# The order of side work in a long-convolution and cosine-gated kernel: table Sin in one row, group matrices by turns, and a tile's sums copied ahead of the preceding Sin

## The chip, the cores and the metric

The kernel runs on one core of a Trainium2 chip. The metric is the device time of one execution in microseconds (us), as the median of several runs. A profile of one execution shows each engine's instructions: TensorE (PE for matmuls, PEld for weight loads), VectorE (DVE), ScalarE (ACT), GpSimd (POOL) and the queue that issues all DMAs (SP).

## What is computed

```python
u = x * v                                    # x, v: 4 x 12480 x 128
h = (np.maximum(pos_emb @ w1, 0) @ w2) * np.exp(-0.01 * pos)[:, None]
y = np.fft.irfft(np.fft.rfft(u, n=2*S, axis=1) * np.fft.rfft(h, n=2*S, axis=0)[None], axis=1)[:, :S]
z = (x * y).reshape(49920, 128)
g = z @ w_in;  g = g * np.cos(g)             # w_in: 128 x 2048
out = g @ w_out                              # w_out: 2048 x 128
```

All is computed in float32. The two gate weights come as float64 and are turned into float32 on the chip.

## The kernel before

**The convolution** is a transform of length 2 x 96 x 120 in two factors, written as matmuls with tables of sines. Its stages are named f1 and f2 (forward), i1 and i2 (inverse). A stage is a Python generator (`units`, L527): for each unit it issues the matmuls, then piece by piece the work that takes the unit before out of PSUM, and the preparation (`before`) of a coming unit. The order in which the instructions are issued is thus written out by hand: the program advances generators in turn (`next`), and every engine carries out its own instructions in exactly that order. A wait at the head of an engine's order holds up all that stands behind it.

**The first 345 us**, up to the first tile of the second part, run in this order:

- the filter h, and its f1 (64 units, matmuls L407, taken out of PSUM by ACT and DVE by turns);
- `first_f1`, the f1 of batch 0: 64 units, evicted by ACT (L415, L423, L425) or DVE;
- `f2_both_units` (L607), the f2 of filter and batch 0 at once: 48 units. Each makes a matrix pair w (`make_w`: ACT L294 scales one term, DVE L296 adds the other), stores it in DRAM (wd) for the later batches, does the matmuls L448 to L454, copies the filter's half out (ACT L633, h), stores that as well (hd), multiplies (DVE L467) and adds (L474, on POOL, but on DVE for the last pair);
- the i1 of batch 0: 64 units, matmuls L479, ACT copies one half (L487, `other`), DVE adds and subtracts it (L489).

Beside them stands work that has to be done some time: the tables of the inverse (`inverse_tables`, L253; POOL computes an argument `turned`, L218, ACT takes its Sin, L227, and the tables are stored as csd, rowsd and twd), the conversion of w_in and w_out to float32 (`convert_units`, L168), and six of the thirty groups of inverse matrices (`some_groups`, L667). PSUM has eight banks in these stages, which units take in turn.

The `Tables` helper lets Sin lag behind their arguments: with a lag of 11 it holds 12 buffers `turned`, and only when 11 arguments wait is the first Sin issued. What is left at the end is issued one Sin at each further step. The steps are driven by f1 and then first_f1, one table step for every fourth of their steps (L873 to L878), so that the last Sin stand between evictions of first_f1.

`beside` (L884) runs the units of a stage, with a convert step at every tenth step (w_in, during first_f1) or every twelfth (w_out, during i1), and a step of `some_groups` where the number of the step modulo 9 is 1 or 5. In front of first_f1 the program advances `f2` once: w of unit 0 is made and stored there, in a pool of its own on the right side.

**The inverse's matrices.** A group is four matrices (`make_group`, L656). A matrix is the sum of two terms: ACT makes the first term (L294); then either DVE multiplies and adds the second (L296), or ACT makes the second into a buffer `spare` (L299) and POOL adds (L300). For the i2 of batch 0, 24 groups are made in the flow, one group ahead, one matrix in each of a unit's four parts: the first two by DVE, the other two by POOL, with one buffer `spare`. The first half of a unit's matmuls (L504) uses the first two matrices. The groups are stored (td) and loaded again by the later batches (`tm<-td`).

**The second part** starts when the first rows of z are there. 98 tiles of up to 512 tokens go through 16 chunks of 128 hidden columns each. For a chunk, `moe_up` (L749) does one matmul into a bank `ph` (L752), ACT makes `a` (L755), DVE rounds it to `k` (L758), POOL subtracts (`f`, L761); `moe_act` (L764) takes the Sin (`cs`, ACT L766) and multiplies by ph (`gt`, DVE L768); `moe_down` (L771) multiplies gt with w_out into the tile's sums `acc` (L777). After a tile's last chunk `moe_evict` copies the sums to `ot` (ACT L783), which is transposed (L127), copied to `ob` (L792) and stored. There are four ph banks and one acc bank; when the convolution is done, odd tiles use another bank (`cv`). The loop (L939 to L961) issues at step i: moe_up of chunk i, moe_act of chunk i - 1, moe_down of chunk i - 4 and, at a tile's end, moe_evict. The rest of the convolution, i2 of batch 0 and then f1, f2, i1, i2 of batches 1 to 3, is fed into the same loop by a budget (`owed`): one step of cost 1 per chunk.

Of the kernel before, what the change touches and what calls it, by code (L numbers as in the profile page):

```python
# [3 lines left out]

# [6 lines left out]
F32 = mybir.dt.float32  # L11
U32 = mybir.dt.uint32
AF = mybir.ActivationFunctionType
# [18 lines left out]
def kernel(  # L32
# [46 lines left out]
    nc = tc.nc  # L79
# [4 lines left out]
    N1, N2 = 96, 120  # L84
    R = S // N2
# [166 lines left out]

    def inverse_tables(pool):  # L253

        t = Tables(pool, nc.gpsimd, 11)
        part = t.whole([P, 1], [[1, 1]], channel_multiplier=1, name="part")
        part4 = t.whole([P, 1], [[1, 1]], base=1, channel_multiplier=4, name="part4")
        step = t.whole([P, P], [[1, P]], name="step")
        mid = t.whole([P, P], [[1, P]], base=-MID, name="mid")
        cs, (rows, tw_t) = third_table(pool), last_tables(pool)  # L260
        yield from t.sines(step, part, N2, [(cs[:, 0, 0:H + 1], 1), (cs[:, 1, 0:H + 1], 0)],
                           eighths=slice(0, H + 1, H))
        yield from t.sines(step[:, 1:H], part, N2,
                           [(cs[:, 0, H + 1:], 0), (cs[:, 1, H + 1:], 1)])
        yield from t.sines(step, part4, 4 * N1,
                           [(rows[:, i, :], q) for i, q in enumerate((0, 1, 2, 3))])
        yield from t.sines(mid, part4, TURN, [(tw_t[:, 0, :], 1), (tw_t[:, 1, :], 0)],
                           eighths=slice(H - 1, N2, H))
        while t.waiting:
            t.finish(1)  # L270
            yield
        for kept, made in ((csd, cs), (rowsd, rows), (twd, tw_t)):
            nc.sync.dma_start(kept[:, :, :], made[:, :, :])

# [27 lines left out]
    def make_w(w, k1, **how):  # L302


        turn(w, even[:, 0, :], even[:, 1, :], tw_w[:, 0, k1:k1 + 1], tw_w[:, 1, k1:k1 + 1],
             **how)
# [149 lines left out]
    def f2_product(pool, ps, h, k1, whole, sums=nc.gpsimd):  # L456
# [12 lines left out]
        for r, op in ((0, ALU.subtract), (1, ALU.add)):  # L469
            if not whole:  # L470
                nc.vector.tensor_tensor(y[:, r], uu[:, 0], h[:, r], op=ALU.mult)
                yield
                nc.vector.tensor_tensor(t[:, r], uu[:, 1], h[:, 1 - r], op=ALU.mult)
            sums.tensor_tensor(y[:, r], y[:, r], t[:, r], op=op)  # L474
            yield

    def i1_mm(ps, b, i):
# [126 lines left out]
            yield from units(N1 // 2, F2_STEPS, before, mm,  # L604
                             lambda j, ps: f2_product(pool, ps, hs.pop(j), 2 * j, False), 4)

    def f2_both_units(bank, w_pool):  # L607

        ws, unkept = {}, []

        def before(j):
            ws[j] = w_pool.tile([KE, 2, N2], F32, name="w")
            for i in range(2):
                make_w(ws[j][:, i, :], 2 * j + i, half=bank)
            unkept.append(j)
            if j < 2:
                keep_w()

        def keep_w():
            while unkept:  # L620
                k = unkept.pop(0)
                nc.sync.dma_start(wd[k, :, :, :], ws[k][:, :, :])

        def mm(j, ps, i):
            if i == 0:
                ps = bank(), bank()
            for filt in range(2):
                f2_mm(ps[filt], ws[j], 2 * j, i, filt=filt == 1)
            return ps

        def after(j, ps):
            h = pool.tile([N2, 2, CB, 4], F32, name="h", bufs=3)
            nc.scalar.activation(h[:, :, :, :].rearrange("p r b j -> p (r b j)"),  # L633
                                 ps[1][0:N2, :], AF.Copy, scale=1.0 / M)
            nc.sync.dma_start(hd[j, :, :, :, :], h[:, :, :, :])
            keep_w()
            yield from f2_product(pool, ps[0], h, 2 * j, True,
                                  nc.vector if 2 * j + 2 == N1 else nc.gpsimd)

        steps = units(N1 // 2, F2_STEPS, before, mm, after, 4, ahead=1)  # L640
        yield next(steps)
        with tc.tile_pool(name="both", bufs=2) as pool:
            yield from steps

    def i1_units(bank):
        with tc.tile_pool(name="mid", bufs=2) as pool:
# [9 lines left out]
    def make_group(pool, g, t, summed, bufs=1):  # L656

        for i, n2 in enumerate(n2s(g)):
            if i < G - summed:
                make_t(t[:, i, :, :], n2)  # L660
            else:
                spare = pool.tile([N1, 2, R], F32, name="spare", bufs=bufs)
                make_t(t[:, i, :, :], n2, spare=spare[:, :, :])
            yield
        nc.sync.dma_start(td[g, :, :, :, :], t[:, :, :, :])

    def some_groups(pool):  # L667
        for g in SOME:
            t = pool.tile([N1, G, 2, R], F32, name="some", bufs=2)
            yield from make_group(pool, g, t, G, bufs=2)  # L670
            if g == SOME[-2]:
                next(backs[0])

    def i2_units(bank, b, bufs):

# [133 lines left out]
    with tc.manual_schedule():  # L809
        with tc.tile_pool(name="psum", bufs=8, space=PSUM) as psum, \  # L810
                ExitStack() as first:
            def bank():
                return psum.tile([P, BANK], F32, name="ps")
# [58 lines left out]
            keep.__exit__(None, None, None)  # L872
            with tc.tile_pool(name="tables", bufs=1) as pool:  # L873
                sines = inverse_tables(pool)
                first_f1 = f1_units(bank, slots[0:R, :, :, :], 0.55)
                for i, _ in enumerate(chain(f1, first_f1)):
                    if i % 4 == 0 and next(sines, "made") == "made":
                        break  # L878

            backs = [inverse_units(lambda: bank(), b) for b in range(B)]

            def beside(units, pieces, every, more=lambda pool: iter(())):  # L884
                with tc.tile_pool(name="convert", bufs=1) as pool:
                    convert, other = convert_units(pool, pieces), more(pool)
                    for i, _ in enumerate(units):
                        if i % every == 0:
                            next(convert, None)
                        elif i % 9 in (1, 5):  # L890
                            next(other, None)
                    for _ in [*convert, *other]:
                        pass

            w_pool = first.enter_context(tc.tile_pool(name="w", bufs=2, side="right"))
# [6 lines left out]
            for _ in f2:  # L902
                pass
            first.close()

# [11 lines left out]
            beside(i1_units(bank), [(w_out_sb[:, c, :], w) for c, w in out_pieces], 12, some_groups)  # L917
# [29 lines left out]
        for i in range(len(steps) + LAG):  # L947
            if i < len(steps):
                n, c = steps[i]
                if n == 0 and c == NFC // 2:  # L950
                    load(1)
                if c == NFC - 4 and n + 2 < NALL:
                    load(n + 2)
                hidden[i] = moe_up(mpool, n, c)
            if 0 <= i - 1 < len(steps):
                gates[i - 1] = moe_act(mpool, *hidden.pop(i - 1))
            if i >= LAG:
                pn, pc = steps[i - LAG]
# [12 lines left out]
            while owed > 0.0:  # L971
                owed -= next(conv, owed)
# [30 lines left out]
```

## Time and profile before

| | |
|---|---|
| median of three runs | 3789.84 us (3787.87 to 3790.01) |
| profiled execution | 3789.84 us, of which the span from the first to the last instruction is 3788.0 us |
| busy: PE, PEld | 3701.4 us (98%), 2105.1 us |
| busy: DVE, ACT, POOL | 2768.3, 2520.8, 2594.0 us |
| mean granted TensorE clock | 0.996 |
| chain that ended last, by engine | PE 81%, POOL 6%, DVE 3%, ACT 2%, DMA 2% |
| DMA | 276.14 MB, mean 73 GB/s |

In the profile, L752 is line 752 of the kernel before. An arrow `cs<-f` names the tile written and the tiles read. Idle time of an engine is put down to what ended it: `PE acc L777 <- ACT ot L783: 9.6, 15, 1.5` means that in 15 places, 9.6 us together and 1.5 us at most, TensorE stood still before an instruction of L777 until ACT had finished an instruction of L783. In the timeline a line gives the start, the time taken, engine, line, operation, tiles and shapes, and in brackets the idle time before. The granted clock is the share of full speed that TensorE got.

### The profile page before, as it was taken

Reading aid. Unit: us, or ns where it says so; the run is one execution under the profiler, and the core shown is the slowest. Engines: PE = TensorE matmul, PEld = TensorE weight load, DVE = VectorE, ACT = ScalarE, POOL = GpSimd, SP = SyncE. Lnnn points to the kernel's source line nnn. Section 1 sums busy time; section 2 is a strip of 40 time slices with the busy share of each in tenths; the row PEclk is TensorE's granted clock in tenths of the full one; section 3 lists DMA queues with packets and bytes.
Section 4 is the critical chain, followed back from the end, with each engine's and each line's share of the span. In section 5 each row is a group of like instructions: output and inputs, shape, how many; then the busy total and the mean of one; then the engine's idle time right before and its main releaser. Section 6 shows DMA issues by size and latency. Waiting matters only on the chain.

```text
span 3788.0 us, 47204 instructions
## 1 busy us (share of the span) xinstructions
PE 3701.4 (98%) x13546; PEld 2105.1 (56%) x13546; DVE 2768.3 (73%) x5564; ACT 2520.8 (67%) x4683; POOL 2594.0 (68%) x2340
## 2 busy tenths in 40 slices
PE   7898999999999999999999999999999999999999
PEld 6776555655466555555565556555566544444444
DVE  7887887688766777778767786788765566666666
ACT  5756776766665557766655567666664677777777
POOL 7666886588854665688745664788644577777776
PEclk9999999999999999999999999999999999999999
DMA  6253452022202651122203540122105300000000
GB/s 166 67 180 100 147 151 60 16 73 76 77 18 66 178 161 27 32 77 77 60 18 109 173 127 18 51 78 76 41 12 164 90 18 22 17 19 21 17 21 14
DMA packets 209498, 276.14 MB, mean 73 GB/s; under 512 B 17111, under 2 KB 146535, under 8 KB 209111
## 3 DMA queue, kind: packets, MB, share of 16 engines
q1 hardware_dynamic: 209239, 273.12, 24.7%
q8 instruction: 109, 1.79, 0.2%
q14 instruction: 150, 1.23, 0.1%
HBM read 193.64 MB, written 79.42 MB: 72 GB/s over the span
## 4 chain that ended last, share of the span: by engine, by line
PE 81%; POOL 6%; DVE 3%; ACT 2%; DMA 2%; issue 2%; SPq 0%; POOLq 0%; DVEq 0%; ACTq 0%
PE ph L752 31%; PE acc L777 26%; PE cv L777 5%; PE cv L504 4%; PE cv L479 4%; POOL f L761 4%; PE cv L407 3%; PE cv L448 3%; PE ph L127 2%; PE ps L448 1%; DMA tm<-td 1%; ACT cs L766 1%; POOL tm L300 1%; DVE k L758 1%; DVE slots L489 1%
## 5 line engine op out<-in xcount | busy, mean ns | idle before, releaser
L761 POOL TENSOR_TENSOR f<-a,k 128x512 f32<-128x512 f32 (+1 forms) x1568 | 1989.0, 1269 | 1055.0 <-DVE k L758 1054.0
L752 PE MATMUL ph<-at,w_in_sb 128*128 128x512 f32 (+1 forms) x3136 | 1598.5, 591 | 5.9 <-DVE gt L768 5.2
L755 ACT ACTIVATE a<-ph,quarter 128x512 f32<-128x512 f32 (+1 forms) x1568 | 1073.3, 685 | 751.7 <-PE ph L752 742.3
L777 PE MATMUL acc<-gt,w_out_sb 128*128 128x512 f32 (+1 forms) x2688 | 1374.1, 593 | 10.0 <-ACT ot L783 9.6
L768 DVE TENSOR_TENSOR gt<-ph,cs 128x512 f32<-128x512 f32 (+1 forms) x1568 | 1077.8, 687 | 319.2 <-ACT cs L766 291.7
L758 DVE TENSOR_SCALAR k<-a 128x512 f32<-128x512 f32 (+1 forms) x1568 | 770.3, 491 | 618.0 <-ACT a L755 598.4
L766 ACT ACTIVATE cs<-f 128x512 f32<-128x512 f32 (+1 forms) x1568 | 980.4, 625 | 338.7 <-POOL f L761 336.3
L777 PEld LDWEIGHTS acc<-gt,w_out_sb 128*128 128x128 f32 x2688 | 505.2, 189 | 663.0 <-issue 619.0
L752 PEld LDWEIGHTS ph<-at,w_in_sb 128*128 128x128 f32 x3136 | 553.5, 190 | 338.2 <-issue 267.0
L474 POOL TENSOR_TENSOR slots<-slots,t 120x256 f32<-120x256 f32 x382 | 309.9, 817 | 63.0 <-DVE t L467 30.8
L504 PEld LDWEIGHTS cv<-slots,tm 96*104 96x104 f32 x1920 | 239.5, 170 | 109.4 <-issue 83.8
L504 PE MATMUL cv<-slots,tm 96*104 96x128 f32 x1920 | 253.7, 274 | 9.7 <-DMA tm<-td 4.9
L777 PE MATMUL cv<-gt,w_out_sb 128*128 128x512 f32 (+1 forms) x448 | 224.5, 583 | 0.7 <-DVE gt L768 0.7
L479 PEld LDWEIGHTS cv<-cs,slots 120*96 120x96 f32 x1536 | 177.5, 168 | 68.0 <-issue 66.1
L479 PE MATMUL cv<-cs,slots 120*96 120x120 f32 x1536 | 183.9, 266 | 0.0
L448 PE MATMUL cv<-slots,w 124*120 124x256 f32 x576 | 173.0, 380 | 0.0
L448 PEld LDWEIGHTS cv<-slots,w 124*120 124x120 f32 x576 | 103.6, 184 | 123.8 <-issue 110.9
L407 PEld LDWEIGHTS cv<-c,slots 104*124 104x124 f32 x768 | 132.5, 192 | 71.2 <-issue 58.3
L407 PE MATMUL cv<-c,slots 104*124 104x192 f32 x768 | 151.2, 326 | 4.8 <-DVE gt L768 3.5
L777 PEld LDWEIGHTS cv<-gt,w_out_sb 128*128 128x128 f32 x448 | 84.9, 190 | 104.5 <-issue 99.5
L395 DVE TENSOR_TENSOR xt<-xt,vt 104x256 f32<-104x256 f32 x177 | 139.1, 793 | 0.8 <-DMA vt<-in_v_dram 0.8
L489 DVE TENSOR_TENSOR slots<-cv,other 96x240 f32<-96x240 f32 x384 | 133.7, 394 | 4.2 <-ACT other L487 4.2
(130 smaller groups left out, 2569.5 us busy)
## 6 DMA issues: line engine op xcount, KB each, us to landing
h<-hd SPq DMA_DIRECT2D x144, 240.0 KB
tm<-td SPq DMA_DIRECT2D x96, 312.0 KB
xt<-in_x_dram SPq DMA_DIRECT2D x120, 208.0 KB
vt<-in_v_dram SPq DMA_DIRECT2D x120, 208.0 KB
xs<-in_x_dram SPq DMA_DIRECT2D x120, 208.0 KB
zd<-zs SPq DMA_DIRECT2D x119, 208.0 KB
zb<-zd SPq DMA_DIRECT2D x96, 256.0 KB
w<-wd SPq DMA_DIRECT2D x144, 116.2 KB
```

The costliest lines, as they stand in the source:

```text
L407: nc.tensor.matmul(ps[0:KE, i * 2 * N1:(i + 1) * 2 * N1], u[:, b, 0:KE, i], c1[0:u.shape[0], :, :].rearrange("p r k -> p (r k)"), start=Tr ...
L448: nc.tensor.matmul(pi, w[:, i, :], parts[0:KE, :, k], start=True, stop=True)
L474: sums.tensor_tensor(y[:, r], y[:, r], t[:, r], op=op)
L479: nc.tensor.matmul(ps[0:N1, (i * 2 + r) * N2:(i * 2 + r + 1) * N2], parts[0:N2, r, :, b, i], cs[:, r, :], start=True, stop=True)
L504: nc.tensor.matmul(ps[0:R, i * D:(i + 1) * D], t[:, i, r, :], slots[0:N1, :, place, :], start=(r == 0), stop=(r == 1))
L752: nc.tensor.matmul(ph[:, 0:m], w_in_sb[:, c * P:(c + 1) * P], ats[n][:, 0:m], start=True, stop=True)
L755: nc.scalar.activation(a[:, 0:m], ph[:, 0:m], AF.Identity, bias=quarter[:, 0:1], scale=INV_TWO_PI)
L758: nc.vector.tensor_scalar(out=k[:, 0:m], in0=a[:, 0:m], scalar1=ROUND, scalar2=ROUND, op0=ALU.add, op1=ALU.subtract)
L761: nc.gpsimd.tensor_tensor(f[:, 0:m], a[:, 0:m], k[:, 0:m], op=ALU.subtract)
L766: nc.scalar.activation(cs[:, 0:m], f[:, 0:m], AF.Sin, scale=TWO_PI)
L768: nc.vector.tensor_tensor(gt[:, 0:m], ph[:, 0:m], cs[:, 0:m], op=ALU.mult)
L777: nc.tensor.matmul(accs[n][:, 0:m], w_out_sb[:, c, :], gt[:, 0:m], start=(c == 0), stop=(c == NFC - 1))
```

## The change

TensorE's instructions keep their order throughout the kernel. What moves is work of the other engines:

1. The inverse tables' lag is 4 instead of 11, with 5 buffers `turned`. The last four Sin are issued in one row. Only f1 drives the steps, every fifth of its steps; the steps left over are all issued behind the last step that f1 yields, and its last two units are evicted behind those; first_f1 follows.
2. w of f2's unit 0 is made at the start of f2, behind first_f1, in the pool of f2's other tiles, again with two buffers. Each w is stored as soon as it is made, ahead of the store of h of the unit before; before, from the third w on, behind it.
3. POOL does the sums L474 of f2's last pair as well.
4. In `beside` a convert step comes at every fourteenth step, and a step of `some_groups` at every fifth. Group 0 of batch 0's i2 is made behind the last of `some_groups`; before, it was made ahead of the last of them.
5. The matrices of a group alternate: DVE, POOL, DVE, POOL. There are two buffers `spare`.
6. In the second part's loop moe_down of chunk i - 4 and the copy of a tile's sums stand ahead of moe_act of chunk i - 1.

```diff
     def inverse_tables(pool):
-        t = Tables(pool, nc.gpsimd, 11)
+        t = Tables(pool, nc.gpsimd, 4)
...
-        while t.waiting:
-            t.finish(1)
-            yield
+        t.finish(len(t.waiting))
...
-            sums.tensor_tensor(y[:, r], y[:, r], t[:, r], op=op)
+            nc.gpsimd.tensor_tensor(y[:, r], y[:, r], t[:, r], op=op)
...
-    def f2_both_units(bank, w_pool):
-        ws, unkept = {}, []
-        def before(j):
-            ws[j] = w_pool.tile([KE, 2, N2], F32, name="w")
-            for i in range(2):
-                make_w(ws[j][:, i, :], 2 * j + i, half=bank)
-            unkept.append(j)
-            if j < 2:
-                keep_w()
+    def f2_both_units(bank):
+        with tc.tile_pool(name="both", bufs=2) as pool:
+            ws = {}
+            def before(j):
+                ws[j] = pool.tile([KE, 2, N2], F32, name="w")
+                for i in range(2):
+                    make_w(ws[j][:, i, :], 2 * j + i, half=bank)
+                nc.sync.dma_start(wd[j, :, :, :], ws[j][:, :, :])
...
-            if i < G - summed:
+            if summed < G and i % 2 == 0:
                 make_t(t[:, i, :, :], n2)
             else:
-                spare = pool.tile([N1, 2, R], F32, name="spare", bufs=bufs)
+                spare = pool.tile([N1, 2, R], F32, name="spare", bufs=2)
                 make_t(t[:, i, :, :], n2, spare=spare[:, :, :])
...
-            yield from make_group(pool, g, t, G, bufs=2)
-            if g == SOME[-2]:
-                next(backs[0])
+            yield from make_group(pool, g, t, G)
+        next(backs[0])
...
-                first_f1 = f1_units(bank, slots[0:R, :, :, :], 0.55)
-                for i, _ in enumerate(chain(f1, first_f1)):
-                    if i % 4 == 0 and next(sines, "made") == "made":
-                        break
+                for i, _ in enumerate(f1):
+                    if i % 5 == 0:
+                        next(sines, None)
+                for _ in sines:
+                    pass
...
-                        if i % every == 0:
+                        if i % 14 == 0:
                             next(convert, None)
-                        elif i % 9 in (1, 5):
+                        elif i % 5 == 0:
                             next(other, None)
...
-            f2 = f2_both_units(bank, w_pool)
-            next(f2)
-            beside(first_f1, [(wind[:, c], w) for c, w in in_pieces], 10)
+            beside(f1_units(bank, slots[0:R, :, :, :], 0.55),
+                   [(wind[:, c], w) for c, w in in_pieces])
...
                 hidden[i] = moe_up(mpool, n, c)
-            if 0 <= i - 1 < len(steps):
-                gates[i - 1] = moe_act(mpool, *hidden.pop(i - 1))
             if i >= LAG:
                 pn, pc = steps[i - LAG]
                 moe_down(pn, pc, gates.pop(i - LAG))
                 if pc == NFC - 1:
                     ots[pn] = moe_evict(mpool, pn)
+            if 0 <= i - 1 < len(steps):
+                gates[i - 1] = moe_act(mpool, *hidden.pop(i - 1))
```

More of the change, by code (lines that the diff above doesn't have):

```diff
@@ L2 @@
 from contextlib import ExitStack
-from itertools import chain
 import concourse.bass as bass
@@ L454, in f2_mm, with f2_product @@
                 nc.tensor.matmul(pi[:, r], w[:, i, :], src, start=True, stop=True)
-    def f2_product(pool, ps, h, k1, whole, sums=nc.gpsimd):
+    def f2_product(pool, ps, h, k1, whole):
         y = parts[0:N2, :, k1:k1 + 2, :, :].rearrange("p r k b i -> p r b (k i)")
@@ L605, in f2_units @@
                              lambda j, ps: f2_product(pool, ps, hs.pop(j), 2 * j, False), 4)
-    def f2_both_units(bank, w_pool):
-        ws, unkept = {}, []
-        def before(j):
-            ws[j] = w_pool.tile([KE, 2, N2], F32, name="w")
-            for i in range(2):
-                make_w(ws[j][:, i, :], 2 * j + i, half=bank)
-            unkept.append(j)
-            if j < 2:
-                keep_w()
[L619 to L641, printed above, removed]
-        with tc.tile_pool(name="both", bufs=2) as pool:
-            yield from steps
@@ new lines, in f2_both_units, with mm, after @@
+    def f2_both_units(bank):
+        with tc.tile_pool(name="both", bufs=2) as pool:
+            ws = {}
[4 more added lines that the diff above has]
+                nc.sync.dma_start(wd[j, :, :, :], ws[j][:, :, :])
+            def mm(j, ps, i):
+                if i == 0:
+                    ps = bank(), bank()
+                for filt in range(2):
+                    f2_mm(ps[filt], ws[j], 2 * j, i, filt=filt == 1)
+                return ps
+            def after(j, ps):
+                h = pool.tile([N2, 2, CB, 4], F32, name="h", bufs=3)
+                nc.scalar.activation(h[:, :, :, :].rearrange("p r b j -> p (r b j)"),
+                                     ps[1][0:N2, :], AF.Copy, scale=1.0 / M)
+                nc.sync.dma_start(hd[j, :, :, :, :], h[:, :, :, :])
+                yield from f2_product(pool, ps[0], h, 2 * j, True)
+            yield from units(N1 // 2, F2_STEPS, before, mm, after, 4, ahead=1)
@@ L654, in i1_units, with make_group @@
                              lambda j, ps: i1_evict(pool, ps, j), 2)
-    def make_group(pool, g, t, summed, bufs=1):
+    def make_group(pool, g, t, summed):
         for i, n2 in enumerate(n2s(g)):
-            if i < G - summed:
+            if summed < G and i % 2 == 0:
                 make_t(t[:, i, :, :], n2)
             else:
-                spare = pool.tile([N1, 2, R], F32, name="spare", bufs=bufs)
+                spare = pool.tile([N1, 2, R], F32, name="spare", bufs=2)
                 make_t(t[:, i, :, :], n2, spare=spare[:, :, :])
@@ L874, with beside @@
                 sines = inverse_tables(pool)
-                first_f1 = f1_units(bank, slots[0:R, :, :, :], 0.55)
-                for i, _ in enumerate(chain(f1, first_f1)):
-                    if i % 4 == 0 and next(sines, "made") == "made":
-                        break
+                for i, _ in enumerate(f1):
[3 more added lines that the diff above has]
+                    pass
             backs = [inverse_units(lambda: bank(), b) for b in range(B)]
-            def beside(units, pieces, every, more=lambda pool: iter(())):
+            def beside(units, pieces, more=lambda pool: iter(())):
                 with tc.tile_pool(name="convert", bufs=1) as pool:
@@ L893, in beside @@
                         pass
-            w_pool = first.enter_context(tc.tile_pool(name="w", bufs=2, side="right"))
-            f2 = f2_both_units(bank, w_pool)
-            next(f2)
-            beside(first_f1, [(wind[:, c], w) for c, w in in_pieces], 10)
+            beside(f1_units(bank, slots[0:R, :, :, :], 0.55),
+                   [(wind[:, c], w) for c, w in in_pieces])
             lpool = ctx.enter_context(tc.tile_pool(name="late", bufs=1))
@@ L901 @@
             nc.sync.dma_start(cs[:, :, :], csd[:, :, :])
-            for _ in f2:
+            for _ in f2_both_units(bank):
                 pass
@@ L916 @@
             nc.sync.dma_start(w_in_sb[:, :], wind[:, :])
-            beside(i1_units(bank), [(w_out_sb[:, c, :], w) for c, w in out_pieces], 12, some_groups)
+            beside(i1_units(bank), [(w_out_sb[:, c, :], w) for c, w in out_pieces], some_groups)
         ps_acc = ctx.enter_context(tc.tile_pool(name="ps_acc", bufs=1, space=PSUM))
```

## The prediction, made before the changed kernel had run

> **What bounds the kernel now.** I read the page first (busy shares, then the chain of work that ended last), then TensorE's busy time by stretches, then the waits, and the timeline where they gather.
>
> ```profile
> PE 3701.4 (98%) x13546; PEld 2105.1 (56%) x13546; DVE 2768.3 (73%) x5564; ACT 2520.8 (67%) x4683; POOL 2594.0 (68%) x2340
> ```
>
> TensorE is busy for 3701.4 of 3788.0 us; 86.6 us of idle time are all that a reordering can win. The stretches show where they lie (columns: length, busy time of PE, PEld, DVE, ACT, POOL, granted clock, DMA share, GB/s):
>
> ```profile
> 110.00:130.00 20.00, 15.73 (x78) 14.56 (x77) 17.10 (x55) 12.76 (x43) 9.55 (x21) 0.83 0.22 65
> 150.00:170.00 20.00, 14.00 (x78) 12.64 (x77) 16.40 (x44) 17.25 (x52) 12.92 (x13) 0.98 0.16 46
> 270.00:285.00 15.00, 11.66 (x110) 11.30 (x110) 7.75 (x23) 6.44 (x19) 7.12 (x12) 1.00 0.55 176
> 320.00:345.00 25.00, 17.29 (x149) 16.34 (x148) 18.96 (x58) 16.79 (x49) 13.58 (x18) 0.96 0.19 57
> 400.00:500.00 100.00, 95.61 (x377) 53.89 (x376) 85.08 (x140) 74.55 (x146) 86.74 (x78) 1.00 0.50 150
> 3000.00:3400.00 400.00, 400.00 (x1019) 182.60 (x1017) 255.04 (x452) 313.18 (x496) 286.78 (x226) 1.00 0.07 19
> ```
>
> After 620 us TensorE hardly rests; before it, every seam between stages costs some us. The change touches three places: the seams up to 345 us (A to D), the stage from 345 to 620 us, where GpSimd is 87% busy in the row of 400-500 us and 85% in 500-600 (E), and each tile's end (F).
>
> **A. The tables' last Sin, and first_f1.** On TensorE's timeline at the seam:
>
> ```profile
> 113.79 2.26 PE L407 MATMUL ps<-c,slots 104*124 104x192 f32 x11
> 116.54 1.57 PE L407 MATMUL ps<-c,slots 104*124 104x192 f32 x8 [0.50 <-ACT slots L415]
> 119.62 1.57 PE L407 MATMUL ps<-c,slots 104*124 104x192 f32 x8 [1.51 <-ACT slots L415]
> 123.42 1.96 PE L407 MATMUL ps<-c,slots 104*124 104x192 f32 x5 [2.23 <-ACT slots L415]
> ```
>
> TensorE loses 0.50 + 1.51 + 2.23 = 4.24 us, because ACT stands before a Sin whose argument GpSimd has not made:
>
> ```profile
> 118.23 0.30 ACT L227 ACTIVATE tw_t<-turned 96x120 f32<-96x120 f32 x1 [1.74 <-POOL turned L218]
> 120.43 0.30 ACT L227 ACTIVATE tw_t<-turned 96x120 f32<-96x120 f32 x1 [0.86 <-POOL turned L218]
> ```
>
> GpSimd makes them at its own pace, the last at 120.4 us. In the changed order the last four Sin stand in a row ahead of ACT's last two evictions of f1, which ended near 111.2 and 112.7 us: the Sin end at 120.7, the evictions near 121.9 and 123.1. first_f1's second unit reuses the first one's bank, so TensorE stops at about 111.7 for 10.2 us in place of 4.24: +6.0. The clock fell to half here already (0.83 in 110-130 us, half from 121.2 to 128.1), so I count that loss as equal. Given back: the convert steps come every 14 units in place of 10, and VectorE is then ahead; TensorE's later stalls in this stage are 0.46 + 0.66 + 0.66 + 0.32 + 1.41 = 3.5 us. 6.0 - 3.5 = **+2.5**, between -1 (150-170 us shrinks by as much again) and +6 (nothing is given back).
>
> [...]
>
> **B. First w.** w0 was made and stored before first_f1; now it follows the last eviction: one ACT term (0.32) and one VectorE sum (0.30) before TensorE can start, **+0.6**, from 0 (TensorE idled 3.6 us here anyway, for ACT slots) to +1.8. The store of w(j+1) now stands in SP's queue ahead of that of h(j-1), no longer behind. From the fourth unit the pace is 2.02-2.04 us, set by a w buffer's store: 3.45 us from issue until the next is made, plus 0.59 us of sums; two buffers as before. The stalls until then, 0.51 and 2.02 us, may grow or go: 0, +-2.
>
> **C. Last pair's sums.** Two on GpSimd (0.72 each, 1.44) where VectorE took 0.91 for both; i1's first matmul at 272.76 waits for them: **+0.5**, to +0.9.
>
> **D. i1 and its company.** ACT waited 6.80 us at 277.54 for tw_t ahead of all copies L487:
>
> ```profile
> 277.54 0.47 ACT L294 ACTIVATE some<-rows,tw_t 96x208 f32<-96x208 f32 x1 [6.80 <-DMA tw_t<-twd]
> 278.64 2.60 DVE L489 TENSOR_TENSOR slots<-ps,other 96x240 f32<-96x240 f32 x8 [5.21 <-ACT other L487]
> ```
>
> Now the table's first use is at i = 5, behind two copies: -1.3 (four L489 at 0.325). Group 0 of i2 (ACT 6 x 0.36-0.46, GpSimd 2 x 0.62) moves from 324 us, inside the stage, to behind its last eviction: +0.5, since TensorE needs about 3 us for the 16 matmuls L504 that come first; up to +3 if it stands before them. Its xs load goes out at about 342 us and must be there at 346.14. Sum **-0.8**, from -2.5 to +3.
>
> **E. Group matrices by turns, two spare buffers (345-620 us).** TensorE's waits there:
>
> ```profile
> PE acc L777 <- ACT ot L783: 5.4, 6, 1.2
> PE ph L752 <- DVE gt L768: 4.4, 7, 1.5
> PE cv L504 <- POOL tm L300: 1.5, 4, 0.6
> PE cv L504 <- DMA tm<-td: 1.4, 1, 1.4
> ```
>
> The work per engine stays: two sums each. ACT's wait for the spare (7.0 us in 12) goes, but ACT is 73-75% busy here and what waits behind it is mostly late for GpSimd's f (1.27 us each). Against it: a group's second matrix, needed with the first by the first half of L504, now comes from GpSimd, one part earlier than GpSimd's first came before. If its margin is gone, each of 24 groups can lose up to a sum (0.89 median). Bounds: -6 (half of these 12.7 us) to +13; nearest row 1.5 us in 4 waits, so **+1**.
>
> ```profile
> L300 POOL TENSOR_TENSOR tm<-tm,spare x48: 616/894/1772, 325.6 to 582.6; 96x208 f32<-96x208 f32 x48
> L300 POOL TENSOR_TENSOR some<-some,spare x24: 619/628/706, 278.4 to 334.3; 96x208 f32<-96x208 f32 x24
> ```
>
> The same sum takes 0.63 us in i1 and 0.89 here. [...]
>
> **F. A tile's sums ahead of the Sin.**
>
> ```profile
> PE acc L777 <- ACT ot L783: 9.6, 15, 1.5
> ```
>
> The next tile's first down matmul waits for the copy ot (0.57), which waited behind a Sin (0.63). These 9.6 us go: 5.4 in 345-620, 4.2 after. The longest, 1.46 at 2694, also brought 3.4 us at half clock: 1.7 more. Of the 5.4, in a stage where GpSimd is next, I keep a quarter as lost: -4.1 - 4.2 - 1.7 = -10.0; other waits take some place (the copy can now hold a Sin that GpSimd was late for), so I take **-7**, between -11.3 and -3. What the move costs is the Sin, 0.43-0.46 us later at a tile's end:
>
> ```profile
> 3425.87 0.57 ACT L783 COPY ot<-acc 128x512 f32<-128x512 f32 x1
> 3426.00 0.69 DVE L768 TENSOR_TENSOR gt<-ph,cs 128x512 f32<-128x512 f32 x1 [0.33 <-ACT cs L766]
> 3427.26 1.02 PE L752 MATMUL ph<-at,w_in_sb 128*128 128x512 f32 x2
> ```
>
> gt ends at 3426.69 and the matmul that reuses its ph starts at 3427.26; a matmul can follow a gt by 0.05, so 0.52 us are free and 0.46 are used. No cost, by 0.06 us; if the weight load (0.19) must also come after gt, 0.14 x 26 tiles of the pure stage = 3.6 us.
>
> **Sum.** +2.5 + 0.6 + 0.5 - 0.8 + 1 - 7 = -3.2 against the profiled execution's 3789.84 (span 3788.0, 1.8 around it), which is also the median of the three runs: **3786.6**.
>
> **Rivals.**
> 1. Slower: GpSimd's earlier matrix. Place: L504's first half in 24 groups. Price: 0.6 us (as the longest L504 wait for tm, 0.6) x 24 = 14 us in place of 1: 3800. It decides once GpSimd's part between two units, f (1.27) plus a sum (0.89), no longer ends before the first half is issued. For it: GpSimd's busy shares, the highest beside TensorE's here. Against: only 1.5 us of such waits now.
> 2. The change does little: F's margin of 0.06 us fails (+3.6) or the 9.6 us reappear as VectorE gt waits, and A gives nothing back: 3790 to 3794.
> 3. All is kept: F -11.3, E -3, A to D 0: 3775.5.
>
> **Chances.** Forecast (3782-3790) 0.42; rival 1 0.22; rival 2 0.18; rival 3 0.18. 0.2% (7.6 us, about what a measurement of this kernel can tell from no change) puts the limits at 3782.3 and 3797.4. Faster: rival 3 and a tenth of the forecast's edge, 0.27; slower: rival 1 and 0.04 of rival 2, 0.26; within 0.47. The range leaves out the far ends of rivals 1 and 3: 3776 to 3802.
>
> **What would show it.** A: one TensorE wait near 10 us for ACT slots at 112-122. B: i1 starting 3 to 4 us later than 272.76. D: L487 copies before the wait for tw_t. E: waits of L504 for tm L300 staying below 3 us; ten or more is rival 1. F: no wait of acc for ot, no half clock at 2694, no new wait of L752 for gt after 3000. I am wrong if i1 starts over 6 us late, or if 345-620 us loses more idle time than the 5.4 of ot.

## The result, and the profile after

The changed kernel took 3774.87 us (median of 4 runs, 3773.07 to 3776.91) against 3789.83 us of the kernel before: a ratio of 0.9962, interval 0.9945 to 0.9979. That is 15 us less; 3 us had been predicted, and the time lies 1 us under the range. The profiled execution took 3773.07 us, its span is 3771.3 us. (Line numbers: L752, L777 and L783 of before are L737, L762 and L768 after; lines of f1 to i2 move up by 3.)

The page's first line, and TensorE's stretches of the same length as those shown of before:

```profile
PE 3694.6 (98%) x13546; PEld 2107.6 (56%) x13546; DVE 2778.8 (74%) x5562; ACT 2517.3 (67%) x4683; POOL 2569.0 (68%) x2342
```

```profile
110.00:130.00 20.00, 12.94 (x62) 12.65 (x62) 11.46 (x38) 10.08 (x37) 9.80 (x19) 0.74 0.17 53
130.00:150.00 20.00, 20.00 (x125) 20.00 (x124) 19.27 (x53) 17.93 (x53) 14.26 (x16) 1.00 0.29 77
270.00:285.00 15.00, 14.38 (x121) 14.19 (x122) 8.77 (x27) 8.19 (x25) 6.85 (x12) 0.89 0.46 150
400.00:500.00 100.00, 95.07 (x361) 52.32 (x360) 87.08 (x139) 70.98 (x143) 75.33 (x76) 0.98 0.50 147
```

110 to 130 us became worse; between 130 and 150 us TensorE is now busy throughout, and i1's first 15 us are better; 400 to 500 us stands as it was. Windows are blunt here, since the work slides past their edges. But TensorE runs the same 13546 instructions in the same order in all of these kernels, so the start of one and the same instruction can be compared. The table is worked out so, from the traces: the time from a stage's first matmul to the next stage's (us), with two exceptions: first_f1 is counted from its second unit (in the changed kernel the first behind TensorE's stop), and i1 from the last matmul of its first unit. The times 620, 2686 and 2701 are those of the first profile of before, and stand for the instruction that starts there; the last column ends with the start of the last matmul. In brackets stands what TensorE lost to half clock in 343-620 at most. That is an estimate from the traces: half of the time for which TensorE was busy there while the granted clock was 0.5. (At f2's start in the kernel before, pairs of matmuls follow each other after 0.85 us at a granted clock of 0.5, and after 0.43 behind it.)

| kernel (run) | start to end of f1 of the filter | first_f1 | f2 | i1 | i2 of batch 0 and beside it, 343-620 | 620-2686 | 2686-2701 | rest |
|---|---|---|---|---|---|---|---|---|
| before | 107.1 | 57.2 | 104.7 | 69.1 | 277.4 (3.4) | 2065.5 | 15.6 | 1082.5 |
| before, again | 107.7 | 56.6 | 104.1 | 68.4 | 276.7 (3.4) | 2064.3 | 15.6 | 1082.5 |
| changed | 114.7 | 49.5 | 102.4 | 64.6 | 279.0 (3.9) | 2056.9 | 12.5 | 1082.4 |
| changed_again | 116.2 | 49.4 | 102.6 | 64.2 | 278.5 (4.0) | 2057.9 | 12.4 | 1082.4 |
| loop_only | 111.5 | 53.5 | 103.8 | 68.8 | 273.8 (0.0) | 2058.4 | 12.6 | 1082.4 |
| tables_only | 119.1 | 51.6 | 102.7 | 68.4 | 277.7 (5.1) | 2064.7 | 14.0 | 1082.6 |
| late_w_again | 108.5 | 55.0 | 102.5 | 67.9 | 279.2 (6.5) | 2063.9 | 14.0 | 1082.5 |
| turns_two_spares | 106.5 | 56.6 | 104.9 | 67.8 | 279.5 (5.1) | 2063.0 | 14.0 | 1082.5 |
| changed_ddpp | 117.6 | 49.4 | 102.8 | 64.2 | 274.5 (2.2) | 2057.0 | 12.5 | 1082.4 |

Two executions of one program (rows 1 and 2, 3 and 4) differ by up to 1.5 us in a stage. The largest change lies behind 620 us, where the prediction had 5.9 us and 10.6 came.

In 343-620 us the half clock differs by more than the edits do. Less the estimate in brackets, the stage takes, in all profiles of this document (D and P are the engines that add a group's four matrices, VectorE and GpSimd; the old loop is that of before, the new one has edit 6):

| order of the matrices | old loop | new loop |
|---|---|---|
| D, D, P, P | 272.1 to 274.0, half clock 3.4 to 6.5 (before, before_again, two_spares, tables_only, beside_i1, convert14, late_w, late_w_again) | 272.1 to 273.8, half clock 0 to 2.2 (loop_only, loop_two_spares, changed_ddpp, ddpp_old_tables) |
| D, P, D, P (by turns) | 274.4 and 275.0, half clock 5.1 and 5.3 (turns_two_spares, changed_old_loop) | 274.4 to 275.2, half clock 3.0 to 9.3 (changed, changed_again, group0_in_flow, loop_turns) |

So at full clock the turns cost about 2 us here with either loop, and edit 6 gives nothing; what the new loop gains in this stage with D, D, P, P is half clock that does not come.

### The profile page after: what moved, and what is told of

Same layout as the page of the kernel before. It is cut to its first block, busy times and chain, and to the rows that moved or that the text cites. A ratio compares the mean times of both kernels' runs of the same rounds, so it can differ in the third digit from the quotient of the medians.

```text
span 3771.3 us, 47191 instructions
## 1 busy us (share of the span) xinstructions
PE 3694.6 (98%) x13546; PEld 2107.6 (56%) x13546; DVE 2778.8 (74%) x5562; ACT 2517.3 (67%) x4683; POOL 2569.0 (68%) x2342
## 4 chain that ended last, share of the span: by engine, by line
PE 87%; DVE 4%; POOL 3%; DMA 2%; ACT 2%; issue 2%; SPq 0%; POOLq 0%; DVEq 0%; ACTq 0%
PE ph L737 33%; PE acc L762 28%; PE cv L762 5%; PE cv L501 5%; PE cv L476 4%; PE cv L445 3%; PE cv L404 3%; PE ph L126 2%; POOL f L746 2%; PE ps L404 1%; PE ps L445 1%; DMA tm<-td 1%; ACT cs L751 1%; DVE slots L486 1%; DVE gt L753 1%
## 5 line engine op out<-in xcount | busy, mean ns | idle before, releaser
L737 PE MATMUL ph<-at,w_in_sb 128*128 128x512 f32 (+1 forms) x3136 | 1599.6, 591 | 8.3 <-DVE gt L753 7.5
L762 PE MATMUL acc<-gt,w_out_sb 128*128 128x512 f32 (+1 forms) x2688 | 1370.4, 591 | 0.0
L743 DVE TENSOR_SCALAR k<-a 128x512 f32<-128x512 f32 (+1 forms) x1568 | 798.0, 509 | 546.8 <-ACT a L740 533.6
L762 PEld LDWEIGHTS acc<-gt,w_out_sb 128*128 128x128 f32 x2688 | 508.3, 189 | 643.0 <-issue 631.7
L737 PEld LDWEIGHTS ph<-at,w_in_sb 128*128 128x128 f32 x3136 | 552.6, 190 | 343.1 <-issue 258.2
L762 PE MATMUL cv<-gt,w_out_sb 128*128 128x512 f32 (+1 forms) x448 | 224.5, 583 | 0.7 <-DVE gt L753 0.7
L762 PEld LDWEIGHTS cv<-gt,w_out_sb 128*128 128x128 f32 x448 | 84.9, 190 | 104.5 <-issue 99.5
## 6 DMA issues: line engine op xcount, KB each, us to landing
w<-wd SPq DMA_DIRECT2D x144, 116.2 KB
```

Source lines behind the costliest of these rows:

```text
L737: nc.tensor.matmul(ph[:, 0:m], w_in_sb[:, c * P:(c + 1) * P], ats[n][:, 0:m], start=True, stop=True)
L743: nc.vector.tensor_scalar(out=k[:, 0:m], in0=a[:, 0:m], scalar1=ROUND, scalar2=ROUND, op0=ALU.add, op1=ALU.subtract)
L762: nc.tensor.matmul(accs[n][:, 0:m], w_out_sb[:, c, :], gt[:, 0:m], start=(c == 0), stop=(c == NFC - 1))
```

## The experiments

All are told as edits of the kernel before or of the changed one. Whole times carry an interval of about 4 us to either side, so the stages carry the verdicts.

**loop_only: edit 6 on the kernel before** (the diff of the loop alone).

> The kernel before, with edit 6 alone (moe_down and the copy of a tile's sums ahead of moe_act). Theory (the waits for the copy were undercounted, since stops of TensorE of a few tenths do not appear in the list of waits): about 11 us less after 620 us and about 6 less in 345 to 620 us, in all -17, near 3773. Rival (the rows of waits were complete and the rest of the gain after 620 us comes from the other edits): -6 after 620 us and up to -5 before, in all -6 to -11, 3779 to 3784.

3777.33 us against 3787.60, ratio 0.9971 (0.9960 to 0.9982). From the table, against the two rows of before: about -3 in 343-620, which is the half clock that both rows of before have and loop_only has not; -6 to -7 in 620-2686; -3 in 2686-2701, of which 1.7 is half clock. The rival fell: 9.6 us of listed waits cannot give this. Summed over the moments at which the next tile's first down matmul starts (from six instructions before it to ten behind it), TensorE gained 6.2 us at the six tile ends before 620 us and 11.1 us behind; half of the first comes back later in that stage. The theory had 17 us in all, 10 came.

What the list of waits had missed shows in one tile's end. Before, TensorE in 1738 to 1742 us:

```profile
1738.40 1.02 PE L752 MATMUL ph<-at,w_in_sb 128*128 128x512 f32 x2
1739.54 1.13 PE L777 MATMUL acc<-gt,w_out_sb 128*128 128x512 f32 x2
1740.51 1.02 PE L752 MATMUL ph<-at,w_in_sb 128*128 128x512 f32 x2
```

After, the same instructions:

```profile
1728.21 1.02 PE L737 MATMUL ph<-at,w_in_sb 128*128 128x512 f32 x2
1729.07 1.02 PE L762 MATMUL acc<-gt,w_out_sb 128*128 128x512 f32 x2
1729.93 1.02 PE L737 MATMUL ph<-at,w_in_sb 128*128 128x512 f32 x2
```

Undisturbed, a pair follows a pair after 0.86 us, though its record is 1.02 long: records of matmuls overlap. Before, the distances are 1.14 and 0.97: 0.28 + 0.11 = 0.39 us lost, and no idle time in brackets. Of the first 0.28 us, 0.16 lie within that overlap (1.02 - 0.86), and the 0.12 us left between the two records (1739.42 to 1739.54) have no bracket. The weight load's record shows the stop, with 0.95 us of idle time. Before:

```profile
1739.54 0.30 PEld L777 LDWEIGHTS acc<-gt,w_out_sb 128*128 128x128 f32 x2 [0.95 <-ACT ot L783]
```

and in the list of who waited for the copy, before, after, and in loop_only:

```profile
  PEld acc L777: 41.0, 45
  PE acc L777: 9.6, 15
```

```profile
  PEld acc L762: 6.7, 26
```

```profile
  PEld acc L777: 8.2, 27
  PE acc L777: 0.3, 1
```

Weight loads waited in 45 places; at 33 of the 97 tile ends loop_only is sooner by over 0.05 us (starts compared as above), where the list of PE has 15. After the change 26 weight loads still wait, for 0.26 us on average, and no matmul does.

**turns_two_spares: edit 5 on the kernel before**, and **two_spares: the second buffer alone**.

```diff
-            if i < G - summed:
+            if summed < G and i % 2 == 0:
...
-                spare = pool.tile([N1, 2, R], F32, name="spare", bufs=bufs)
+                spare = pool.tile([N1, 2, R], F32, name="spare", bufs=2)
```

> The kernel before, with edit 5 alone (matrices D, P, D, P and two buffers spare). Theory (the turns cost time in 345 to 620 us, which ate the gain of edit 6 there): +5 to +8 us, all of it in 345 to 620 us, near 3796. Rival (the turns are free; the gain of edit 6 in that stage was given back because GpSimd was next): within 1.5 us of the kernel before.

> The kernel before, with a second buffer spare alone, the order D, D, P, P kept. Theory (the cost of edit 5 lies in the order of the turns): -2 to +1 us. Rival (it lies in the second buffer, which lets ACT run ahead into terms while its Sin wait): +4 to +8 us, as with the turns.

3788.08 against 3787.60 us (ratio 0.9992 to 1.0011) and 3784.98 (0.9986 to 1.0005): as whole times, within their intervals. In 343-620 us the turns took 279.5, 2 to 3 more than before, less than the theory's 5 to 8; the second buffer alone took 275.6, 1 to 2 less. So the order costs, not the buffer: less the half clock, these two kernels take 274.4 and 272.2. In the whole times the rival of the turns held (+0.5).

**changed_ddpp: the changed kernel with the order D, D, P, P**, two buffers kept.

```diff
-            if summed < G and i % 2 == 0:
+            if summed < G and i < 2:
```

> The changed kernel, with the order D, D, P, P of the matrices and two buffers spare: all its edits but the turns. Theory (the order of the turns costs about 4 us in 345 to 620 us, the second buffer gives about 2): 3 to 4 us faster than the changed kernel, 3771. Rival (what the stage loses comes from GpSimd being full, whichever order): no change, 3775.

3771.51 us, 3.4 under the first measurement of the changed kernel and 1.2 under the second (3772.70), both measured apart from it; its ratio to before, 0.9960 (0.9947 to 0.9972), is that of the changed kernel (0.9962 and 0.9961), so the whole times show no difference. In 343-620 us it takes 274.5 against 279.0 and 278.5, so 4.3 us less. The theory holds in the stage: the order of the turns costs about 4 there, of which 1.8 is half clock. TensorE's waits in 340 to 620 us, changed kernel first (the changed kernel's loop has no wait for ot left):

```profile
PE ph L737 <- DVE gt L753: 6.4, 8, 1.4
PE cv L501 <- DMA tm<-td: 4.4, 3, 2.3
PE cv L501 <- POOL tm L297: 2.3, 6, 0.6
```

```profile
PE ph L737 <- DVE gt L753: 5.7, 8, 1.5
PE cv L501 <- DMA tm<-td: 3.1, 2, 1.6
PE cv L501 <- POOL tm L297: 1.1, 3, 0.6
```

Each is a little longer with the turns, by 3.2 together; the wait for GpSimd's matrix, which the prediction's first rival had at 14, accounts for 1.2. The transfers' part does not repeat: the row has 3.6 in changed_again and 3.7 in ddpp_old_tables, which has D, D, P, P. GpSimd's sums are not slower with the turns: none takes more than 0.82 us in the changed kernel, while some take up to 1.77 in changed_ddpp. Why gt is later, and what makes up the rest, was not separated.

**loop_turns and loop_two_spares: edit 6 on the kernel before, with edit 5 or with the second buffer alone.**

> The kernel before, with edits 5 and 6 alone. Theory (in 345 to 620 us the costs of both add up: edit 6 alone gave 3.6 us there, the turns alone took 2.1): 1 to 2 us less in that stage, near 3777 in all. Rival (they get in each other's way, as GpSimd is full): no gain in the stage or a loss, 3779.

> The kernel before, with edit 6 and a second buffer spare, the order D, D, P, P kept. Theory (they add up: 3.6 + 1.8): 5 us less in 345 to 620 us, near 3774, and 3 to 4 us under edits 5 and 6 together. Rival (the second buffer gives nothing once the copy stands first): 3777, as with edits 5 and 6 together.

3776.52 us (ratio 0.9960 to 0.9981) and 3775.20 (0.9956 to 0.9979). In 343-620 us loop_two_spares takes 273.8, as loop_only does, so its theory of 5 us less fell; but 1.7 of it is half clock, of which loop_only has none, so whether the second buffer still gives 1 to 2 us stays open. loop_turns' profile shows 283.7 there, 9.3 of it half clock (13.7 us at half clock begin at 341.8 us, 6.8 us more at 437.4), and that execution was some 10 us over the median of its kernel; its whole time shows no difference to loop_only that can be told. Less the half clock it takes 274.4, as the turns alone do: at full clock the cost of the turns is the same with both loops.

**group0_in_flow: the changed kernel with group 0 where it was.**

```diff
-            yield from make_group(pool, g, t, G)
-        next(backs[0])
+            yield from make_group(pool, g, t, G)
+            if g == SOME[-2]:
+                next(backs[0])
```

> The changed kernel, with group 0 of batch 0's i2 made ahead of the last of some_groups again, as before the change. Theory (group 0 at the end of i1 costs TensorE the 4.9 us wait for its matrix, of which making it in the flow takes back about 2 us): first matmul of i2 about 2 to 3 us sooner, in all 3772. Rival (the work costs the same wherever it stands, since i1 is held by its evictions): no change, 3775.

3776.52 us (0.9960 to 0.9979 of before). i1 took 66.4 us where the changed kernel has 64.6 and 64.2: the old place is 2 us worse, so the theory has the wrong sign. The 4.9 us for which TensorE waits at the end of i1 in the changed kernel,

```profile
336.20 4.99 PE L501 MATMUL cv<-slots,tm 96*104 96x128 f32 x24 [4.88 <-DVE tm L293]
```

are mostly i1's own last evictions: the kernel before has 3.10 there, and group0_in_flow 4.63, both put down to the sums of i1. That the group, made in the flow, delays the evictions that set i1's pace is argued from the 2 us; no run shows it by itself.

**beside_i1: the rhythm beside i1 alone**, on the kernel before.

```diff
-                        elif i % 9 in (1, 5):
+                        elif i % 5 == 0:
...
-            beside(i1_units(bank), [...], 12, some_groups)
+            beside(i1_units(bank), [...], 14, some_groups)
```

> The kernel before, with the changed rhythm beside i1 alone (convert at every fourteenth step, some_groups at every fifth); group 0 stays where it was. Theory (some_groups' first step no longer holds ACT for the table's load ahead of all copies): first matmul of i2 2 to 3 us sooner, counted from the first of i1; the rest as before. Rival (the gain in i1 came with group 0's move, which takes its terms out of ACT's and VectorE's way): less than 1 us.

3787.45 against 3786.69 us (0.9993 to 1.0011); i1 took 66.7 us, 2 less than before (69.1, 68.4). The theory holds in the stage, too small for the whole time. In the changed kernel ACT waits for the table once, with the first copies done:

```profile
271.97 0.35 ACT L484 COPY other<-ps 96x240 f32<-96x240 f32 x1 [3.81 <-PE ps L476]
273.09 0.35 ACT L484 COPY other<-ps 96x240 f32<-96x240 f32 x1 [0.76 <-PE ps L476]
274.59 0.47 ACT L291 ACTIVATE some<-rows,tw_t 96x208 f32<-96x208 f32 x1 [1.15 <-DMA tw_t<-twd]
```

1.15 us in place of 6.80.

**tables_only: edit 1 on the kernel before**, and **convert14: a convert step at every fourteenth step of first_f1, alone.**

```diff
-            beside(first_f1, [(wind[:, c], w) for c, w in in_pieces], 10)
+            beside(first_f1, [(wind[:, c], w) for c, w in in_pieces], 14)
```

> The kernel before, with edit 1 alone (lag 4, steps driven by f1 alone, the last four Sin in one row); convert steps stay at every tenth. Theory (the 10 us stop was given back because convert steps stand further apart): the first matmul of f2 comes 3 to 6 us later than before, 3792. Rival (TensorE catches up without that, since after a stop the evictions are ahead of it): 0 to 1 us later, 3788.

> The kernel before, with a convert step at every fourteenth step of first_f1 in place of every tenth, and nothing else. Theory (TensorE's stops of 3.5 us in the stage come from convert steps too close to each other): first matmul of f2 2 to 4 us sooner, 3785. Rival (as many pieces are converted, so as much is lost): no change within 1 us.

tables_only: 3791.48 against 3786.69 us, ratio 1.0011 (1.0002 to 1.0020); f2's first matmul came 6.3 us later than in the first profile of before. convert14: 3789.12 us (0.9990 to 1.0009); f2's first matmul came 3.4 us sooner, and f2 itself took 107.4 us, 3 more. Both theories hold at f2's start: edit 1 alone is a loss, and the wider steps give time back. In the whole time convert14 won nothing. TensorE in the changed kernel, then tables_only, in first_f1:

```profile
119.64 44.81 PE L404 MATMUL ps<-c,slots 104*124 104x192 f32 x252 [7.06 <-ACT slots L412]
```

```profile
129.04 14.57 PE L405 MATMUL ps<-c,slots 104*124 104x192 f32 x88 [0.27 <-ACT slots L413]
143.78 3.84 PE L405 MATMUL ps<-c,slots 104*124 104x192 f32 x20 [0.17 <-DVE slots L415]
147.96 3.85 PE L405 MATMUL ps<-c,slots 104*124 104x192 f32 x20 [0.35 <-DVE slots L415]
152.51 3.83 PE L405 MATMUL ps<-c,slots 104*124 104x192 f32 x20 [0.70 <-DVE slots L415]
```

With a step every 14, all 252 instructions behind the stop run without another; with one every 10, TensorE stops five more times between 143 and 161 us (three are shown), every 20 instructions, which is one convert step.

**ddpp_old_tables: the changed kernel with D, D, P, P and with edit 1 undone.**

> The changed kernel with the order D, D, P, P (two buffers spare) and with edit 1 undone: lag 11, the last Sin among first_f1's evictions. Theory (edit 1 costs 3 to 5 us that the wider convert steps do not fully give back, since f2 behind it then runs sooner): 3768, 3 us under the changed kernel with D, D, P, P. Rival (f2's pace is held by the stores of w, and what first_f1 gains is lost there): 3771, no change against it.

3769.63 us; the changed kernel, measured beside it, 3772.70; ratios to before 0.9952 (0.9940 to 0.9965) and 0.9961 (0.9948 to 0.9973). It is the fastest of all, by 1.9 us under changed_ddpp, which was measured apart from it; that is too little to tell. In its profile TensorE is 6.6 us sooner than before late in first_f1, and then waits:

```profile
169.06 1.18 PE L448 MATMUL ps<-slots,w 124*120 124x256 f32 x2 [10.52 <-DVE w L296]
```

f2 starts at 169.1 us, as in the changed kernel (169.13) and before (168.89). VectorE's row tells what w0 waits for:

```profile
168.62 1.09 DVE L296 SCALAR_TENSOR_TENSOR w<-even,tw_w,ps 124x120 f32<-124x120 f32 x4 [3.44 <-DMA wind<-power]
```

So it is not the stores of w that take the gain away here, but the store of the last converted piece of w_in, which has to land before w0 is made. In the changed kernel w0 waits for ACT's term instead (2.73 us), which stands behind the last evictions; so the theory was not put to a fair test. Whether edit 1 costs anything in the changed kernel stays open: f2 starts at 169.1 us here, at 169.1 and 170.2 in the two profiles of the changed kernel, and at 171.9 in changed_ddpp.

**late_w: edit 2 on the kernel before**, run twice, the second time with **before_again**.

> The kernel before, with w of f2's unit 0 made at the start of f2 and each w stored as it is made (edit 2 alone). Theory (the start is later by two sums, but the stall of the first units goes, since w0's and w1's buffers are stored in time): first matmul of f2 1 us later, the 22nd unit's 1 to 3 us sooner, no change of the time within 2 us. Rival (the wait for the store is the same whoever starts it): later by 1 to 2 us throughout.

> Edit 2 alone again, on one chip with the kernel before itself. Theory (edit 2 takes away the stall of f2's first units at the price of 0.7 us at its start): 1 to 3 us under the kernel before; from f2's first matmul to the 24th pair of units 1 to 2 us less than in the kernel before of the same call. Rival (the first measurement's 5 us are its own): 4 to 6 us under.

> The kernel before itself, for a second profile and for how far two executions of one program lie apart in the seams. Theory (the half-clock stretches fall differently in each execution, and the stall of f2's first units varies): first matmul of the second part within 3 us of the first profile, but not the same, the stall at the 7th unit of f2 0.4 to 1.5 us in place of 2.0; time as before within 0.1%. Rival (the seams repeat): every milestone before 345 us within 0.5 us.

late_w: 3782.87 against 3788.01 us (0.9978 to 0.9996). late_w_again: 3783.77 against 3786.88 (0.9983 to 1.0000). f2 took 101.7 and 102.5 us, against 104.7 and 104.1 of before: 2 us less. Its first matmul came 0.7 us later, counted from the last quarter of first_f1. VectorE's queue shows where: before, then late_w, the wait of the seventh w for its buffer's store:

```profile
183.82 0.59 DVE L296 SCALAR_TENSOR_TENSOR w<-even,tw_w,ps 124x120 f32<-124x120 f32 x2 [2.23 <-DMA wd<-w]
```

```profile
179.27 0.59 DVE L296 SCALAR_TENSOR_TENSOR w<-even,tw_w,ps 124x120 f32<-124x120 f32 x2 [0.22 <-DMA wd<-w]
```

TensorE's waits for a w in f2, before, then late_w:

```profile
PE ps L448 <- DVE w L296: 3.8, 5, 2.0
```

```profile
PE ps L448 <- DVE w L296: 1.3, 3, 0.6
```

In before_again they are 3.3, at most 1.1; in late_w_again 1.3, at most 0.8. before_again came out at 3786.55 us; its milestones up to 343 us lie within 1.35 us of the first profile. There the same w waits 1.27 us, and its row puts that down to ACT's copy of h and not to the store, so how much of the stall the store alone makes is not shown. Up to 1 us of the gain is a difference between executions, and the 5 us of the first whole time are not edit 2's alone.

**changed_old_loop: the changed kernel with edit 6 undone**, beside **changed_again**.

> The changed kernel itself, to stand beside the next three on one chip. Theory (edit 6 gives about 10 us, the other edits together 1 to 3): 12 us under the kernel before. Rival (the first comparison's 15 us are exact and the other edits give 4 to 5): 15 us under.

> The changed kernel with edit 6 undone: edits 1 to 5 alone. Theory (edit 6 is nearly all of the gain): 0 to 3 us under the kernel before. Rival (edit 6 gives what the list of waits showed, 6 to 7 us, and the seams the rest): 6 to 8 us under the kernel before.

3772.70 and 3782.52 us, before, measured beside them, 3788.01: ratios 0.9961 (0.9948 to 0.9973) and 0.9988 (0.9979 to 0.9997). Edit 6 is worth 9.8 us of 15.3, the other edits together 5.5. Behind 620 us edit 6 gives 9.3 us here (2065.2 and 14.0 us in changed_old_loop, against the two rows of the changed kernel), with no half clock there in any of the three profiles. Here the truth lies between: edit 6 gives what its theory says, the rest what the rival says.

## Why the prediction was wrong, step by step

- **F failed, as a size: 7 predicted, 10 measured in whole times, 13 in the stages of loop_only.** "These 9.6 us go" took the list's row for TensorE as the whole. It holds 15 stops; 33 tile ends became shorter. Behind 620 us the gain is 10.6 us (table, 7.5 + 3.1), where 5.9 stood; without half clock it is 9.3 (changed_old_loop), where 4.2 stood. In 343-620 us, where 4.1 stood, edit 6 gives nothing at full clock; the half clock falls by 3.5 us on average with D, D, P, P and not at all with the turns. That the -10.0 worked out before a part was held back meets the 10 of the whole times is luck: it is too small behind 620 us and too large before. The 1.7 us for the half clock near 2694 is in part chance: the wait of 1.46 us stands in all ten profiles with the old loop, the half clock in four of them (15.6 in that column, else 14.0), and in none of the eight with the new loop. That the Sin costs nothing at the end held: the last column is 1082.4 to 1082.6 us in every row. The margin of 0.06 us was enough.
- **A: right in its place, too dear.** The stop came, but took 7.06 us, not 10.2: GpSimd was done with the last argument at 118.1 us, not 120.4. The half clock lasted 10.2 us from 115.3, of which 5.9 lie behind the stop. Up to first_f1's second unit TensorE lost 8 us, and first_f1 returned 7.4 (4.24 of that are the stops that the kernel before has inside first_f1): about +0.6 with w0's later start in it, where A and B had +3.1. That convert steps would give part of it back was right: convert14 shows it.
- **B: the start right, the stalls at the edge of their range.** The start is later by 0.7, predicted 0.6. "The stalls until then, 0.51 and 2.02 us, may grow or go: 0, +-2" gave the store's new place in SP's queue no value: f2 became 2 us shorter, and TensorE's waits for w fell by 2.0 to 2.5 us.
- **C: right.** TensorE's wait ahead of i1 is 3.1 us in the changed kernel, against 2.66 before and 2.7 in late_w, where VectorE still makes the sums: +0.4, predicted 0.5.
- **D: wrong by a factor of 5:** -4.3, predicted -0.8, outside its range. The rhythm gave 2.0 (predicted 1.3), and group 0's move gave another 2 where I had charged 0.5. The reading that fits is that i1 is held by ACT's copies and VectorE's sums, so what leaves their queue is gained there, while TensorE's wait at i1's end grew only by 1.8 us (4.88 against 3.10).
- **E: sign right, size wrong:** +4.3, predicted +1: about 2 at full clock, the rest half clock. The wait that was named, of L504 for GpSimd's matrix, makes up 1.2 of it; the rest has no shown cause.
- **The sum by the table** (mean of two profiles each): up to f2's start +0.6, f2 -1.9, i1 -4.3, 343-620 +1.7, behind -10.6, in all -14.6. The prediction had +3.1, +0.5, -0.8 and, for the last two together, -6: it was too high by 2.5, 2.4, 3.5 and 3.0 us, so no single term explains the miss of 11.4. F's error, the largest behind 620 us (4.7), is half hidden in the sum by what E cost and F did not give in 343-620.
- **Rivals.** Rival 1 (slower) did not come: 2.3 us of waits of L504 for tm, not 14. Rival 3 (3775.5) has the right time for the wrong reasons: it had A to D at 0, which came to -5.6, and E at -3, which came to +4.3.

## What to carry to other kernels

Where the records of matmuls overlap, as here (1.02 us long, 0.86 us apart), read a wait from the distance of starts or from the weight loads' rows, not from TensorE's idle time alone: here 15 stops were listed and 33 tile ends became shorter. When two kernels keep TensorE's order, compare the start of the same instruction; it separates edits of 2 us that whole times with 4 us of interval cannot. First take off what the half clock took: in 343-620 us that was 0 to 9.3 us and hid which edit gave what. In i1, which seems to be held by its evictions, work taken out of their queue was gained (2 us by the rhythm alone, 2 us by group 0's move), even where the same work then stood at the stage's end.

## What the runs showed of the hardware

TensorE's half clock (granted clock 0.5) came in lengths of 3.4, 6.8, 10.2 and, in convert14 and loop_turns, 13.7 us, a stretch that begins in the kernel's last microsecond left aside, and did not fall the same way in two executions: near first_f1's start it began at 121.2 us and lasted 6.8 in the first profile of before, at 124.3 and 3.4 in the second. What sets these lengths and starts, no run shows. The prediction counted one such stretch near 2694 us as an effect of the copy's wait: the wait was there in every run with the old loop, the half clock only in four of ten. Two executions of one program differed by 0.8 to 1.3 us at i2's first matmul (before, the changed kernel and late_w, two profiles each); how much of that is the half clock and how much the landing of stores was not separated.
